# A list-scheduled attention and feed-forward kernel: a third engine allowed for two kinds of cast, and a new table of places

## The chip, the core and the metric

The kernel runs on one core of a Trainium2 chip. A core has a matrix engine (TensorE, PE in the rows; its weight loads are PEld), a vector engine (VectorE, DVE), a scalar engine (ScalarE, ACT), GpSimd (POOL), and SyncE (SP), which here only issues DMAs. Each engine works through its own list of instructions in order; semaphores tie the lists together. The metric is the device time of one execution in microseconds (us), the median of several. A profiled execution gives a trace, and its span (first to last instruction) is a little shorter than its device time.

## What is computed

```python
scores = q @ k.T / 8                    # 8 batches x 8 heads, 576 tokens, 64 wide
# heads 0-3 keep the 32 tokens up to their own, heads 4-7 every 32nd token
attn = softmax(where(mask, scores, -1e9)) @ v
x = attn.transpose(0, 2, 1, 3).reshape(4608, 512)
h = x @ w_in                            # 512 x 2048
out = (h * sigmoid(h)) @ w_out          # 2048 x 512
```

## The kernel before, in words

Attention is split per batch into six groups: groups 0 to 2 hold tiles of the local heads, 3 to 5 tiles of the strided heads. A group's steps are: load of keys and queries (`k`), scores on PE (`S`), masked copy with the row's peak on DVE (`M`, line 574), exponential on ACT (`E`, 583 or 595), row sums and scaling on DVE (`R`, `N`), a turn on PE and a copy back on ACT (`T`, `P`), the product with the values on PE (`O`), and the copy of its result into x on ACT (`B`, 686 or 703). In later batches the turn is done by a DMA with two 16-bit copies ahead of it (`X`) and two behind it (`Z`), which any of DVE, ACT and POOL may make (lines 638 and 648).

The feed-forward part keeps float32 accuracy with pairs of fp32r numbers, an upper part and a remainder. The weights come as 32 pieces of 512 KB (16 of w_in, 16 of w_out, taken in turn). A piece costs one load `p`, two ACT passes that round it (`a`, lines 434 and 439), a joining DVE pass (`j`, 445), a cast of the upper part (`b`, 481), and a DVE subtraction for the remainder (`d`, 485). x gets the same: a cast of each of its four quarters (`H`, 722) and a subtraction (`L`, 727). The first three blocks of 512 tokens are multiplied straight (`h` and `o`, lines 735 and 782); the other six go in three pairs by a scheme with fewer products, whose combined operands DVE and ACT make (products at lines 1598 and 1637).

Nobody writes the order of the instructions down. Each piece of work is a `Step` with a cost for every engine that may do it and a due time. `Steps.arrange` (line 294) simulates the engines: among the steps that can begin next it takes the one with the earliest due time, and of the engines that a step may use, the one on which it would end first. The order found is the order of every engine's list. Two tables correct it: `SHIFT` adds to the due time of single steps, `GIVEN` pins single steps to one engine. The order of the DMA issues on SP comes out of the same due times, so the first loads can be read from the code: due of a `k` load of batch 0, group c, is -1 + 2.2c, of a `v` load 6 + 2.2c, of a weight load 14 + 6.4(fc + 1.4 layer), each plus its entry in `SHIFT`; the earliest is issued first.

Of the kernel before, what the change touches and what calls it, by code (L numbers as in the profile page):

```python
# [25 lines left out]
B, H, S, D = 8, 8, 576, 64  # L26
# [48 lines left out]
class Group:  # L75
# [50 lines left out]


SHIFT = {
# [52 lines left out]
}  # L181
GIVEN = {
# [5 lines left out]
}  # L188


# [159 lines left out]
def sparse_attention_ffn(ctx: ExitStack, tc: tile.TileContext, kqt, vt, w_in, w_out, out, out_t):  # L350
# [453 lines left out]
    add = steps.add  # L804
    state = {}

    def do(*args, **kwargs):
        return steps.do(*args, **kwargs)
# [173 lines left out]
    def piece_steps(i):  # L982
        layer, fc = pieces[i]
        due = begin + (fc + layer * 1.4) * pace - 4
        lent_to = []
        if fc in cuts[layer][0]:
            lent_to = [lent[key] for half in range(2) if (key := (layer, half, fc)) in lent]
        if i % AHEAD < LENT and i < 2 * (NFC - LENT):
            where = f"stage{i % AHEAD}"
        else:  # L990
            where = f"ring{next(turns) % (AHEAD - LENT)}"
        p = add(f"p{i}", {"SP": 512 * P * 8 / RATE}, due - 6, [], lambda: load_piece(i),
                writes=[where])
        a = add(f"a{i}", {"ACT": 1.18}, due, [p], lambda: round_weights(stages[i]))
        j = add(f"j{i}", {"DVE": 0.7}, due + 0.5, [a], lambda: join_weights(stages[i]))
        h = add(f"b{i}", {"DVE": 0.46, "ACT": 0.57}, due + 1, [j],
                lambda: high(i, h.engine), writes=lent_to)
        d = add(f"d{i}", {"DVE": 0.66}, due + 1.5, [h], lambda: low(i))
        steps.reads(d, where)
        return d  # L1000
# [2 lines left out]

    def x_steps(k, cc, after=(), due=None):
        more = 0.2 * (((k + 1) * T - 1) // S - k * T // S)
        high = do(f"H{k}{cc}", {"ACT": 0.52 + more, "DVE": 0.5 + more},
                  lambda: x_high(k, x, cc, high.engine), writes=[("x", cc)], after=after, due=due)
        low = do(f"L{k}{cc}", {"DVE": 0.68 + 0.5 * more},
                 lambda: x_low(k, x, cc, low.engine), writes=[("x", cc)], due=due)
        return high, low  # L1010
# [878 lines left out]
```

## Time and profile before

| | |
|---|---|
| time, median of 3 runs | 816.59 us (815.8 to 817.57) |
| the profiled execution | 814.57 us, span 812.8 us |
| PE busy in the span | 795.9 us (98%) |
| DVE, ACT, POOL busy | 571.2, 474.1, 58.8 us |
| DMA | 190.21 MB, mean 234 GB/s |

Busy time of PE is the time in which a product was under way; its pauses are the span less that. The stretches and single rows that matter are in the section of rows below.

### The profile page before, as it was taken

The numbers are of one execution on the slowest core, as the hardware profiler recorded it, in microseconds if no ns is written. First come the engines' busy times: TensorE is split into PE (matmuls) and PEld (weight loads), VectorE is DVE, ScalarE is ACT, GpSimd is POOL, SyncE is SP. The second block draws the span as 40 slices with busy tenths as digits, with TensorE's granted clock in tenths as the row PEclk, the third lists the DMA queues.
The fourth block names the chain that finished last, engine by engine and source line by source line (L and its number), as shares of the span: only waits on it lengthen the run. The fifth ranks groups of instructions, "written<-read, shape, count | busy, mean of one in ns | idle before, by whom it ended". The sixth has DMA issues, their size and how long they took to land.

```text
span 812.8 us, 17610 instructions
## 1 busy us (share of the span) xinstructions
PE 795.9 (98%) x6900; PEld 655.7 (81%) x6900; DVE 571.2 (70%) x1370; ACT 474.1 (58%) x1160; POOL 58.8 (7%) x67
## 2 busy tenths in 40 slices
PE   5899999999999999999999999999999999999997
PEld 4788888888888888887888888888888888888886
DVE  6999876768988988843898866237867640379662
ACT  7988754636566656777678554555545344455440
POOL 2000000012100112100221100000000000000000
PEclk9999999999999999999999999999999999999999
DMA  9898988878776888889887778665585675555662
GB/s 330 298 299 243 243 237 257 254 212 241 223 236 181 251 257 251 243 256 264 275 269 257 257 263 278 198 220 182 184 230 187 238 244 177 194 207 191 205 225 103
DMA packets 112979, 190.21 MB, mean 234 GB/s; under 512 B 42880, under 2 KB 87424, under 8 KB 102144
## 3 DMA queue, kind: packets, MB, share of 16 engines
q1 hardware_dynamic: 112896, 189.08, 73.3%
q8 instruction: 54, 0.88, 0.4%
q14 instruction: 29, 0.24, 0.1%
HBM read 141.08 MB, written 38.80 MB: 221 GB/s over the span
## 4 chain that ended last, share of the span: by engine, by line
PE 95%; DMA 2%; ACT 2%; DVE 0%; SPq 0%; issue 0%; DVEq 0%
PE z L1637 28%; PE z L1598 27%; PE po L782 16%; PE ph L735 16%; PE pa L555 3%; PE ph L668 1%; DMA w<-ops 1%; PE z L668 1%; DMA w<-kqt 1%; PE pa L668 1%; ACT stage L434 0%; ACT stage L439 0%; PE po L668 0%; SPq L492 0%; ACT xhi L722 0%; ACT pt L618 0%
## 5 line engine op out<-in xcount | busy, mean ns | idle before, releaser
L1598 PE MATMUL z<-w,w 128*128 128x512 f32 x720 | 166.5, 390 | 0.8 <-DMA w<-ops 0.8
L1598 PEld LDWEIGHTS z<-w,w 128*128 128x128 f32 x720 | 134.8, 188 | 29.3 <-issue 1.2
L1637 PE MATMUL z<-w,w 128*128 128x512 f32 x576 | 133.9, 389 | 0.0
L1637 PEld LDWEIGHTS z<-w,w 128*128 128x128 f32 x576 | 108.0, 188 | 22.5
L735 PE MATMUL ph<-xhi,w 128*128 128x512 f32 x384 | 123.8, 392 | 0.0
L583 ACT ACTIVATE sm<-sm,sums 128x64 f32<-128x64 f32 x304 | 101.5, 340 | 9.2 <-DVE sums L574 8.2
L782 PE MATMUL po<-w,g 128*128 128x512 f32 x432 | 104.3, 392 | 0.0
L782 PEld LDWEIGHTS po<-w,g 128*128 128x128 f32 x432 | 80.3, 188 | 17.4 <-DVE g L762 0.5
L1464 DVE TENSOR_TENSOR w<-w,w 128x1024 fp32r<-128x1024 f32 (+3 forms) x68 | 78.3, 1162 | 12.2 <-ACT w L1535 9.6
L735 PEld LDWEIGHTS ph<-xhi,w 128*128 128x128 f32 x384 | 72.3, 188 | 15.4
L735 PE MATMUL ph<-xlo,w 128*128 128x512 f32 x192 | 75.0, 390 | 0.0
L1493 DVE TENSOR_TENSOR w<-w,z 128x1024 f32<-128x1024 f32 x30 | 36.5, 1218 | 37.4 <-PE z L1598 37.3
L1535 ACT CAST w<-w 128x1024 fp32r<-128x1024 f32 (+1 forms) x40 | 39.2, 987 | 35.5 <-PE z L1637 34.1
L583 ACT ACTIVATION_READ_ACCUMULATOR sm<-sm,sums 128x1 f32 x304 | 58.6, 193 | 0.0
L1481 ACT ACTIVATE w<-w 128x1024 f32<-128x1024 f32 x30 | 31.8, 1062 | 39.8 <-DVE w L1493 39.7
L648 POOL COPY pt<-sm 128x896 uint16<-128x896 uint16 (+1 forms) x21 | 28.7, 1375 | 322.9 <-DMA sm<-pt 233.4
L1637 PE MATMUL z<-xhi,w 128*128 128x512 f32 x216 | 52.0, 390 | 0.0
L1637 PE MATMUL z<-xlo,w 128*128 128x512 f32 x216 | 52.0, 390 | 0.0
L1487 ACT COPY w<-z 128x1024 f32<-128x1024 f32 x30 | 30.4, 1014 | 35.5 <-PE z L1598 35.4
L745 ACT ACTIVATE th<-ph 128x512 f32<-128x512 f32 x48 | 28.5, 593 | 37.3 <-DVE g L762 24.2
L1637 PEld LDWEIGHTS z<-xhi,w 128*128 128x128 f32 x216 | 40.5, 188 | 8.5
L1637 PEld LDWEIGHTS z<-xlo,w 128*128 128x128 f32 x216 | 40.5, 188 | 8.4
(169 smaller groups left out, 1173.3 us busy)
## 6 DMA issues: line engine op xcount, KB each, us to landing
w<-ops SPq DMA_DIRECT2D x84, 1024.0 KB, 4.9
ops<-stage SPq DMA_DIRECT2D x48, 256.0 KB, 3.1
kd<-kqt SPq DMA_DIRECT2D x23, 448.0 KB, 5.6
ops<-w SPq DMA_DIRECT2D x80, 128.0 KB, 4.2
vd<-vt SPq DMA_DIRECT2D x24, 384.0 KB, 6.0
stage<-w_out SPq DMA_DIRECT2D x16, 512.0 KB, 5.3
stage<-w_in SPq DMA_DIRECT2D x16, 512.0 KB, 6.4
kd<-kqt SPq DMA_DIRECT2D x14, 442.0 KB, 5.5
```

Of the source, the lines that this page charges most:

```text
L583: nc.scalar.activation(out=self.s_sb[:, c, r], in_=self.s_sb[:, c, r], func=AF.Exp, bias=self.nmax[:, c, r : r + 1], scale=-1.0, accum_out ...
L648: copy[engine](out=self.halves(self.pt)[:, half], in_=came[:, half])
L735: nc.tensor.matmul(ph, weight(0, wi, fc)[:, cc * P : (cc + 1) * P], x[xi][:, cc], start=(cc, n) == (0, 0), stop=(cc, n) == (NP - 1, 2),)
L745: nc.scalar.activation(out=th[:, cols], in_=ph[:, cols], func=AF.Tanh, scale=0.5)
L782: nc.tensor.matmul(po[tt], g[gi][:, cols], weight(1, wi, fc), start=fc == 0 and n == 0, stop=fc == NFC - 1 and n == 2,)
L1464: nc.vector.tensor_tensor(out=o, in0=x, in1=y, op=op1)
L1481: nc.scalar.activation(out=o, in_=x, func=AF.Silu)
L1487: nc.scalar.copy(out=o, in_=x)
L1493: nc.vector.tensor_add(o, x, y)
L1535: nc.scalar.copy(out=hi, in_=x)
L1598: nc.tensor.matmul(zt[z][:, jj], w[:, at, wi, cc * P : (cc + 1) * P], op[:, xi, cc], start=fresh and (cc, n) == (0, 0), stop=(cc, n) == (1 ...
L1637: nc.tensor.matmul(zt[zz][:, ds], w[:, at, wi, ds * P : (ds + 1) * P], op[:, gi, jj], start=fresh and (jp, jj, n) == (0, 0, 0), stop=(jp, ...
```

## The change

The casts of the weights' upper parts (`b`, 32 steps) and of x (`H`, 12 steps) may now go to POOL as well; the schedule takes 0.95 us and 0.9 us (plus a little where a block crosses batches) for them there. Steps with two operands are not offered to POOL. `SHIFT` and `GIVEN` are replaced as a whole, so nearly every step may stand at another place. What the schedule does not hold is any cost of one engine's work to another engine.

```diff
 SHIFT = {
...
-    "j2": 237, "j21": 1761.5, "k": -132.5, "k0.0": -132.5, "k1.1": -7497.23, "k10.1": 121, "k12.3": 231,
-    "k13.1": 229.5, "k14.2": 247, "k14.5": 275.5, "k15.0": 277, "k16.4": 309, "k2.2": -7499.41,
-    "k20.5": -337.5, "k21.0": -300, "k21.3": -138, "k22.4": -123, "k23.2": -163, "k3.3": -6873,
-    "k4.4": -34, "k5.5": -7513.5, "k6.3": -37, "k7.1": 19.5, "k7.4": 60.5, "k8.5": 75.5, "k9.0": 144.5,
...
-    "o7": 161.5, "p1": -132, "p10": 30.5, "p11": -2.5, "p12": 51.5, "p13": 47.5, "p14": 46.5, "p15": 56,
...
-    "p4": -144.5, "p5": -48.5, "p8": 44.5, "plain0.0.A110": -47.5, "plain0.0.A120": -44,
...
+    "E6.4": 2299, "E7.6": 2354, "H12": 2338.5, "L01": 2089.5, "L12": 2246.5, "L13": 1556,
+    "M1.1": 1646.5, "M1.2": 1687, "M19.1": 2259.5, "M19.3": 2210.5, "M19.4": 2259.5, "M19.5": 2224.5,
...
+    "h12": -427.5, "h13": -418, "h14": -428.5, "h2.6": -562.5, "h2.7": 208.5, "i1.15": -477,
...
+    "j8": 2362, "j9": 2403.5, "k": -2836.5, "k0.0": -1354.5, "k1.1": -1393.5, "k10.1": 70, "k10.4": 117,
+    "k13.1": 202, "k15.3": -247.5, "k16.1": 393, "k2.2": -2911.5, "k21.3": -72.5, "k3.3": -1581,
+    "k4.4": -339.5, "k5.5": -1011, "k6.0": -224, "k6.3": -183.5, "k7.1": -333, "k7.4": -185,
...
+    "l2.10": 2353, "l2.5": -348, "l8": 1858, "o1.11": -502.5, "p0": -202, "p1": -1306, "p10": -114.5,
+    "p11": -89, "p12": -121, "p16": 54.5, "p17": 39, "p2": -408, "p20": 45.5, "p21": 38, "p23": 33,
+    "p24": 38.5, "p3": -186, "p4": -335.5, "p5": -179.5, "p6": -138, "p7": -281, "p8": -196.5,
+    "p9": -147.5, "plain0.0.A110": -278, "plain0.0.A111": -299, "plain0.0.A220": 46.5,
...
+    "q1.3": -345, "s0.1": 274, "s0.2": 265, "t1.3": 2159, "v0.0": -263.5, "v1.1": -374, "v12.0": 283,
...
+    "v3.3": -215, "v4.4": -228, "v5.5": -366, "v7.1": -134, "w1.15": -770, "w15": 2316, "w2.0": -376.5,
...
 }
 GIVEN = {
-    "H02": "DVE", "H13": "ACT", "H23": "DVE", "X13.1": "ACT", "X16.0": "ACT", "X19.0": "ACT",
-    "X6.1": "POOL", "X7.0": "ACT", "Z12.0": "POOL", "Z12.1": "POOL", "Z14.0": "ACT", "Z16.0": "DVE",
-    "Z18.0": "DVE", "Z6.0": "ACT", "b16": "DVE", "b17": "ACT", "b18": "ACT", "b19": "ACT", "b2": "ACT",
-    "b20": "ACT", "b23": "ACT", "b26": "ACT", "b5": "ACT", "b8": "DVE", "w2": "ACT", "w2.10": "ACT",
-    "w2.2": "DVE", "w3": "ACT", "w5": "DVE",
+    "H01": "POOL", "H13": "POOL", "X11.1": "ACT", "X13.0": "ACT", "X14.1": "ACT", "X15.0": "POOL",
+    "X16.0": "POOL", "X6.1": "POOL", "X7.0": "ACT", "X7.1": "ACT", "Z17.1": "POOL", "b0": "POOL",
+    "b12": "POOL", "b13": "ACT", "b19": "ACT", "b27": "POOL", "b3": "POOL", "b31": "POOL", "b4": "DVE",
+    "b8": "ACT", "b9": "ACT", "w1.0": "DVE", "w2": "ACT",
 }
...
-        h = add(f"b{i}", {"DVE": 0.46, "ACT": 0.57}, due + 1, [j],
+        h = add(f"b{i}", {"DVE": 0.46, "ACT": 0.57, "POOL": 0.95}, due + 1, [j],
                 lambda: high(i, h.engine), writes=lent_to)
...
-        high = do(f"H{k}{cc}", {"ACT": 0.52 + more, "DVE": 0.5 + more},
+        high = do(f"H{k}{cc}", {"ACT": 0.52 + more, "DVE": 0.5 + more, "POOL": 0.9 + more},
                   lambda: x_high(k, x, cc, high.engine), writes=[("x", cc)], after=after, due=due)
```

## Rows read from the trace of the kernel before

**Rows 1.** Busy time by stretch (stretch, its length, each engine's busy time and instructions, clock, DMA).
```profile
0.00:6.40 6.40, 1.89 (x72) 1.46 (x72) 0.02 (x1) 1.28 (x1) 4.74 (x24) 1.00 0.61 206
6.40:14.00 7.60, 3.86 (x131) 2.89 (x131) 6.56 (x64) 6.85 (x38) 0.00 (x0) 1.00 1.04 377
14.00:20.00 6.00, 5.39 (x93) 4.11 (x96) 5.63 (x22) 6.00 (x18) 0.00 (x0) 1.00 1.06 399
20.00:32.80 12.80, 10.14 (x280) 8.42 (x275) 12.18 (x39) 12.26 (x30) 0.00 (x0) 1.00 0.84 281
40.00:100.00 60.00, 60.00 (x552) 49.06 (x551) 55.08 (x149) 50.00 (x136) 2.88 (x2) 1.00 0.91 265
100.00:380.00 280.00, 279.97 (x3025) 230.87 (x3023) 213.26 (x684) 171.87 (x564) 31.57 (x26) 1.00 0.81 240
380.00:382.00 2.00, 1.20 (x6) 0.72 (x5) 1.22 (x1) 0.10 (x1) 0.00 (x0) 1.00 0.93 264
382.00:808.20 426.20, 426.20 (x2731) 352.31 (x2729) 269.69 (x389) 219.28 (x356) 19.65 (x15) 1.00 0.66 219
```
**Rows 2.** Timeline of PE: start, duration, instruction, idle time before and what ended it.
```profile
4.06 0.92 PE L555 MATMUL pa<-w 64*64 64x64 f32 x24 [4.06 <-DMA w<-kqt]
5.35 0.97 PE L555 MATMUL po<-kd 64*32 64x64 f32 x48 [0.36 <-DMA kd<-kqt]
...
29.75 1.12 PE L668 MATMUL po<-pt,w 64*64 64x54 f32 x32 [1.05 <-ACT pt L618]
30.79 2.03 PE L555 MATMUL pa<-kd 64*32 64x64 f32 x80
32.76 0.79 PE L735 MATMUL ph<-xhi,w 128*128 128x512 f32 x1
...
381.41 1.86 PE L1598 MATMUL z<-w,w 128*128 128x512 f32 x7 [0.80 <-DMA w<-ops]
```
**Rows 3.** The chain that ended last, 13 to 30 us (start, duration, what).
```profile
17.52 0.56 ACT stage L434
18.08 0.57 ACT stage L439
...
25.10 0.55 ACT w L481
...
27.56 0.62 ACT xhi L722
...
29.21 0.49 ACT pt L618
```
**Rows 4.** Timelines of POOL, DVE and ACT at the start.
```profile
0.96 2.27 POOL L390 TENSOR_SCALAR_AFFINE_SELECT mask_local<-mask_local 32x64 f32<-32x64 f32 x8
...
6.38 0.22 DVE L574 CUSTOM_DVE_ANT_0 sm<-pa,mask_strided 128x64 f32<-128x64 f32 x1 [6.38 <-POOL mask_strided L390]
...
6.64 0.35 ACT L583 ACTIVATE sm<-sm,sums 128x64 f32<-128x64 f32 x1 [4.63 <-DVE sums L574]
```
**Rows 5.** DMA issues of the first 40 us: KB each, median us from issue to landing.
```profile
kd<-kqt SPq DMA_DIRECT2D x5, 448.0 KB, 5.9
...
w<-kqt SPq DMA_DIRECT2D x1, 334.0 KB, 3.3
...
stage<-w_in SPq DMA_DIRECT2D x7, 512.0 KB, 8.5
```
**Rows 6.** Groups of casts, 6.4 to 32.8 us (count, busy us, mean ns of one, idle before).
```profile
L481 ACT CAST w<-stage 128x512 fp32r<-128x512 f32 x3 | 2.0, 663 | 0.0
L722 ACT CAST xhi<-xb 128x512 fp32r<-128x512 f32 x3 | 1.9, 619 | 0.1
...
L481 DVE CAST w<-stage 128x512 fp32r<-128x512 f32 x3 | 1.3, 426 | 0.1
L722 DVE CAST xhi<-xb 128x512 fp32r<-128x512 f32 x1 | 0.4, 419 | 0.0
```
**Rows 7.** Copies on POOL: durations ns min/median/max, and one small copy.
```profile
L638 POOL COPY pt<-sm x22: 827/1172/2026, 53.0 to 522.4; 128x896 uint16<-128x896 uint16 x15, 128x768 uint16<-128x768 uint16 x7
...
3.30 0.24 POOL L403 COPY mask_first<-mask_local 128x72 f32<-128x72 f32 x1
```
**Rows 8.** DVE beside a POOL copy (timelines), and one DVE line's durations min/median/max.
```profile
107.24 1.29 POOL L648 COPY pt<-sm 128x768 uint16<-128x768 uint16 x1 [13.84 <-DMA sm<-pt]
107.53 1.49 DVE L485 TENSOR_TENSOR stage<-stage,stage 128x512 fp32r<-128x512 f32 x1
...
L762 DVE TENSOR_TENSOR g<-th,g x48: 629/691/1520, 39.3 to 321.7; 128x512 fp32r<-128x512 f32 x48
```
**Rows 9.** Casts of weights, 33 to 130 us, by engine.
```profile
L481 ACT CAST w<-stage 128x512 fp32r<-128x512 f32 x13 | 8.5, 659 | 0.6 <-DVE stage L445 0.6
...
L481 DVE CAST w<-stage 128x512 fp32r<-128x512 f32 x10 | 4.2, 424 | 0.2
```

77 rows, old and new, of the table SHIFT are left out of this document.

## The prediction

> **What bounds the kernel now.** I read the busy time by stretch first, because the shares of a whole span hide where an engine waits. From 32.8 us to 808.2 us PE pauses only once for long, 0.80 us at 381 us for a load [rows 1, 2]; all other stretches there are busy to within 0.03 us. The products themselves are not touched by this change, so they cannot get shorter. What can get shorter is the time in which PE waits: the span less its busy time is 812.8 - 795.9 = 16.9 us. Of this, 32.8 - (1.89 + 3.86 + 5.39 + 10.14) = 11.5 us lie before the first big product at 32.76 us [rows 1, 2], 0.8 us at 381 us, and 4.6 us behind the last product, where nothing of the change has a place. So the question is what sets the start of the big products.
>
> The first 4.06 us are the wait for the first load [rows 2]. Behind it, ACT and DVE are both nearly full: ACT 6.00 of 6.00 us and 12.26 of 12.80, DVE 5.63 and 12.18 [rows 1]. The chain of work that ended last says which of the two counts more. It lies on ACT for most of 13.2 to 29.7 us: roundings, a weight cast, casts of x, and last the copy of 29.21 us, for which PE waits 1.05 us before the last batch-0 attention product at 29.75 us [rows 2, 3]. POOL has nothing to do from 6.4 us to beyond 32.8 us [rows 1].
>
> **The change, part by part.** *Casts that leave ACT and DVE.* Between 6.4 and 32.8 us there are six casts on ACT and four on DVE [rows 6]. One of the six, a weight cast, starts at 32.43 us, too late to matter. A cast keeps ACT for 0.55 us (25.10 us in the chain; its 0.66 us overlaps its neighbour), and DVE for 0.43 us [rows 3, 6]. The table pins b0, b3 and H01 to POOL and b4 to DVE; the others go where they would end first, and with both other engines over 95% full that will often be POOL although it is slower. I take six of the ten: four from ACT, 4 x 0.55 = 2.2 us, two from DVE, 0.85 us. Ends: three and nine.
>
> *What a cast costs on POOL.* No row of before has a 512-wide float32 copy there. The nearest are 0.24 us for 72 wide and 0.83 us for the quickest 768-wide 16-bit copy [rows 7]; on the line between, 512 wide takes 0.24 + 440 x 0.59/696 = 0.61 us. Float32 at twice the stride may be slower: the upper end is the median of the 16-bit copies, 1.17 us, some of which were held back. I take 0.8 us, nearer to the lower end, whose rows nothing held back. Against ACT's 0.55 us that is up to 0.25 us more on one dependence, hidden where the next step waits for ACT anyway. [...]
>
> *What POOL does to DVE.* At 107.53 us a DVE subtraction of two operands takes 1.49 us, where that line's neighbours take 0.69: it began 0.29 us after a POOL copy and ended only after it [rows 8]. The same happens to the line with 48 instructions, 0.691 us in the median and 1.520 at worst [rows 8]. So a POOL copy can hold DVE back by anything from nothing to 0.83 us. I take 0.4 us a cast, halfway, since a copy may start at any point of a DVE instruction: 6 x 0.4 = 2.4 us on DVE. The schedule counts none of this. [...]
>
> *The order of the first loads.* Before, group 5 came first; it needs the mask for strided heads, for which DVE waits until 6.38 us, though PE had begun at 4.06 us [rows 2, 4]. By the new due times the order is k2, k (first tile of group 0), k3, k1, k0, v2, p1, k5. Group 2 needs only the local mask, finished at 0.96 + 2.27 = 3.23 us [rows 4]. Its load is 114 KB bigger than group 5's [rows 5], 0.3 us at 377 GB/s [rows 1], so PE begins at about 4.4 us, its 48 products take 0.97 us [rows 2], and DVE and ACT begin about 1.0 us earlier. The loads behind come no faster, since the DMA engines were full before too (1.04 and 1.06 of their time [rows 1]), so some of this runs into waits for data: I take 0.7 us on both engines. Ends: 0 and 1.6 us.
>
> *Together before 32.8 us.* ACT: -0.7 - 2.2 = -2.9 us. DVE: -0.7 - 0.85 + 2.4 = +0.85 us. The chain lies on ACT far more than on DVE, but DVE is close behind; I weigh them 0.8 to 0.2: -2.3 + 0.2 = -2.1 us for the start of the stream.
>
> *The stream, 33 to 130 us.* Here 23 more weight casts are made on w, 10 of them on DVE [rows 9]. If some 13 go to POOL, five of them from DVE, DVE gets 13 x 0.4 - 5 x 0.43 = +3.1 us. It has 4.9 us free between 40 and 100 us alone [rows 1], so I count nothing; without that cover (13 x 0.83 - 2.1 = 8.7 us, against 4.9) PE would wait 3.8 us. The new places of all later steps I cost at nothing too: after 100 us DVE is busy 213 of 280 us and ACT 172 [rows 1], and PE hides them; the 0.80 us at 381 us may go or double, with no row that says which.
>
> **Sum.** 812.8 - 2.1 = 810.7 us of span. The profiled execution's own time was 814.57, so 812.5 us there; the median of the runs lies 2.0 us above the profiled one, and 816.59 - 2.1 gives 814.5 us.
>
> **Rivals.** *Both engines freed.* If POOL takes nine casts (five of ACT, 2.7 us, and all four of DVE, 1.7 us) and finds gaps on DVE, ACT is 0.7 + 2.7 = 3.4 us earlier, or 4.3 us with all of the 1.6 us of the first loads; about 4 us gives 812.6 us. For it: POOL is empty. Against: DVE leaves few gaps.
>
> *DVE takes the bound (slower).* Place: DVE's two-operand passes before 32.8 us and up to 100 us. At 0.6 us a cast, six casts put DVE 3.6 - 1.55 = 2.05 us later before the stream, and in it 13 casts cost 7.8 - 2.1 = 5.7 us, 0.8 us more than DVE has free: +2.9 us, 819.4 us, once the chain has moved to DVE. At the worst price, 0.83 us, it is 3.4 + 3.8 = +7.2 us. It decides where DVE's delay before the stream is zero, 1.55/6 = 0.26 us a cast, if DVE sets the start alone, and at some 0.58 us, where the free time is used up, if ACT does. For it: the 1.49 us row; against: the median of that line in the trace stays at 0.69 us.
>
> *The loads set the start, and the change hides.* The piece of w_in that the first product needs lands late: issued at 15.36 us before, with 8.5 us to landing [rows 5] that is near 24 us, and in the new order p0 stands behind a like amount of data. Three microseconds of rounding, joining, cast and subtraction follow, so before 27 us nothing can start; PE then still has the last attention and the next scores to do, 1.12 + 2.03 us [rows 2], which it does in any order. If attention also waits for its values, a gain of -0.5 us stays: 816.1 us. That is also where the change would end if few casts moved.
>
> **Chances.** A difference under 0.2% (1.6 us) is about what a measurement of this kernel cannot tell from none. My forecast (-1.0 to -3.2 us) 0.42, of which 0.35 is over 0.2%; both freed 0.14; loads 0.20, of which 0.03 is a gain over 0.2%; DVE bound 0.24, of which 0.19 is over 0.2% slower. Faster 0.52, same 0.29, slower 0.19. The range from 811.5 to 818.5 us reaches from the second-best part of "both freed" to the milder part of "DVE bound" and leaves out under 2 in 10; the forecast's own range is 813.4 to 815.6 us.
>
> **What would show it.** Right: POOL casts of about 0.8 us between 17 and 32 us, fewer casts on ACT there, DVE's first mask before 5.6 us, the first big product at 30 to 31.5 us, PE without pauses behind it, DVE passes of 1.0 to 1.5 us beside POOL casts. Wrong: big products that start at 32.5 us or later, pauses of PE between 40 and 130 us that end with a DVE subtraction, or a longer wait near 381 us.

## The result: 820.44 us, slower by half a per cent

The changed kernel takes 820.44 us (median of 6 runs, 819.43 to 823.06). The kernel before took 816.58 us beside it. The ratio is 1.0054, 95% interval [1.0041, 1.0066]: slower, where 814.5 us and a gain had been forecast. The profiled execution took 820.87 us, its span is 818.7 us.

Below `GIVEN` all line numbers are ten lower than before: the cast of a weight is L471 (was L481), of x L712 (722), the subtractions L475 and L717, the first product of the stream L725, the gate passes of the feed-forward part L739 and L752. Kernels built from before keep the old numbers.

Busy time by stretch, the columns as in [rows 1]:

```profile
0.00:6.40 6.40, 1.18 (x64) 0.94 (x64) 1.04 (x13) 2.06 (x6) 4.74 (x24) 1.00 0.67 195
6.40:14.00 7.60, 4.27 (x139) 3.40 (x139) 5.80 (x50) 6.02 (x31) 0.00 (x0) 1.00 1.04 388
14.00:20.00 6.00, 5.38 (x143) 4.75 (x135) 5.57 (x22) 6.00 (x21) 1.77 (x2) 1.00 0.85 328
20.00:32.80 12.80, 8.11 (x200) 6.40 (x197) 9.99 (x33) 8.74 (x23) 2.69 (x3) 1.00 0.92 313
40.00:100.00 60.00, 59.95 (x477) 48.78 (x476) 54.09 (x141) 44.56 (x124) 8.57 (x9) 1.00 0.86 270
100.00:380.00 280.00, 275.61 (x3074) 225.91 (x3073) 222.44 (x683) 165.73 (x542) 42.85 (x42) 1.00 0.78 236
380.00:382.00 2.00, 2.00 (x11) 1.65 (x10) 0.00 (x0) 2.00 (x13) 0.84 (x1) 1.00 0.79 287
382.00:812.00 430.00, 429.77 (x2747) 355.23 (x2745) 270.86 (x389) 230.99 (x369) 19.85 (x14) 1.00 0.65 221
```

PE's busy time is 795.7 us, as before. Its pauses are 818.7 - 795.7 = 23.0 us, where they were 16.9 us [rows 1]. The 6.1 us more are: up to 32.8 us 13.86 instead of 11.52 us (+2.3); from 100 to 380 us 280 - 275.61 = 4.39 instead of 0.03 us (+4.4); the wait at 381 us is gone (-0.8); 0.2 us behind that. These are two single executions. The one of before lies 2.0 us below its median and this one 0.4 above, so 6.1 us of the profiles stand for 3.9 us of the medians.

Where the pauses are, in the timeline of PE:

```profile
27.01 1.12 PE L658 MATMUL po<-th,w 64*64 64x54 f32 x32 [3.91 <-DMA w<-vt]
...
33.93 0.50 PE L725 MATMUL ph<-xhi,w 128*128 128x512 f32 x1
...
42.27 2.88 PE L772 MATMUL po<-w,g 128*128 128x512 f32 x12
...
117.16 0.55 PE L658 MATMUL pa<-pt,vd 64*64 64x32 f32 x24 [0.38 <-ACT th L735]
127.77 0.50 PE L725 MATMUL ph<-xlo,w 128*128 128x512 f32 x1 [0.56 <-DVE xlo L717]
163.93 0.56 PE L658 MATMUL ph<-pt,vd 64*64 64x54 f32 x21 [1.16 <-issue]
214.02 0.50 PE L725 MATMUL ph<-xhi,w 128*128 128x512 f32 x1 [0.57 <-DVE th L739]
239.20 0.50 PE L725 MATMUL ph<-xhi,w 128*128 128x512 f32 x1 [0.54 <-DVE th L739]
321.88 0.50 PE L725 MATMUL ph<-xhi,w 128*128 128x512 f32 x1 [1.19 <-DVE th L739]
```

The first big product starts at 33.93 us, 1.17 us later than before [rows 2]. The block of 36 products that it opens ends at 42.27 us, 0.71 us later than before (41.56 us): here the products stand 0.23 us apart from the second on, while in before the first two took 0.59 and 0.42 us. The longest wait before the first big product, 3.91 us, is for values of batch 0. The chain that ended last says why they are late, and the waits of SP's queue confirm it:

```profile
16.17 1.19 POOL w L471
...
17.39 1.12 DVE w L475
...
18.56 0.38 SPq L460
...
18.98 0.86 SPq L489
...
19.88 6.99 DMA w<-vt
```

```profile
SPq L460 <- DVE w L475: 6.9, 1, 6.9
```

SP issues the loads in the order of its list: L460 at 18.56 us, and only then, at 18.98 us, L489. At 11.6 us SP comes to the load of weight piece 7 (L460), whose buffer DVE gives back only with the subtraction for piece 1, at 18.51 us. Two loads of values (L489) stand behind it. The DMA engines run dry meanwhile: from 19 to 20 us they are busy for 0.26 of the time, where it was 1.07 in before. Two windows of after, then the same two of before (DMA share and GB/s are the last columns):

```profile
18.00:19.00 1.00, 1.00 (x50) 1.00 (x44) 1.00 (x2) 1.00 (x6) 0.00 (x0) 1.00 0.63 246
19.00:20.00 1.00, 1.00 (x44) 1.00 (x40) 0.93 (x5) 1.00 (x3) 0.00 (x0) 1.00 0.26 72
```

```profile
18.00:19.00 1.00, 1.00 (x44) 1.00 (x44) 0.96 (x3) 1.00 (x4) 0.00 (x0) 1.00 1.07 409
19.00:20.00 1.00, 0.68 (x27) 0.54 (x26) 1.00 (x6) 1.00 (x5) 0.00 (x0) 1.00 1.07 419
```

Three of the later pauses end with the same DVE instruction, L739. DVE and POOL ahead of the one at 214 us:

```profile
208.39 0.69 DVE L1149 TENSOR_TENSOR stage<-w,w 128x512 f32<-128x512 f32 x1 [1.43 <-DMA ops<-stage]
209.11 0.42 DVE L1159 TENSOR_TENSOR stage<-stage 128x256 f32<-128x256 f32 x1
...
210.03 1.40 DVE L1161 TENSOR_TENSOR stage<-stage 128x256 f32<-128x256 f32 x1
...
212.28 1.09 DVE L595 TENSOR_TENSOR sm<-sm,sums 128x896 f32<-128x896 f32 x1
213.29 0.68 DVE L739 SCALAR_TENSOR_TENSOR th<-th,ph 128x512 f32<-128x512 f32 x1
```

```profile
210.00 1.20 POOL L638 COPY pt<-sm 128x896 uint16<-128x896 uint16 x1 [4.88 <-DMA sm<-pt]
```

DVE waits 1.43 us until a store empties a buffer, then makes sums for the product scheme. One of them takes 1.40 us instead of 0.42, from 0.03 us behind the start of a 16-bit join on POOL to 0.23 us behind its end. Only then comes the gate pass that PE needs. Nothing in this chain is a cast on POOL: the join, `Z12.0`, was pinned to POOL in the old `GIVEN` too and stands at another moment now. In all, POOL makes 46 of the 16-bit copies, where it made 43.

### The profile page after: what moved, and what is told of

It reads as the page before. It is cut to its first block, busy times and chain, and to the rows that moved or that the text cites. A ratio compares the mean times of both kernels' runs of the same rounds, so it can differ in the third digit from the quotient of the medians.

```text
span 818.7 us, 17658 instructions
## 1 busy us (share of the span) xinstructions
PE 795.7 (97%) x6900; PEld 654.4 (80%) x6900; DVE 578.1 (71%) x1361; ACT 473.3 (58%) x1145; POOL 82.0 (10%) x95
## 4 chain that ended last, share of the span: by engine, by line
PE 78%; DVE 11%; DMA 4%; ACT 3%; issue 2%; SPq 0%; POOL 0%; DVEq 0%; ACTq 0%; POOLq 0%
PE z L1627 28%; PE z L1588 26%; PE po L772 10%; PE ph L725 9%; PE pa L545 3%; DMA ops<-stage 2%; ACT sm L573 1%; DVE th L739 1%; PE ph L658 1%; DVE stage L435 1%; DMA w<-vt 1%; DVE w L475 1%; DVE g L752 1%; PE z L658 1%; DVE stage L1177 1%
## 5 line engine op out<-in xcount | busy, mean ns | idle before, releaser
L725 PE MATMUL ph<-xhi,w 128*128 128x512 f32 x384 | 123.9, 392 | 2.3 <-DVE th L739 2.3
L725 PEld LDWEIGHTS ph<-xhi,w 128*128 128x128 f32 x384 | 72.1, 188 | 18.9 <-DVE th L739 3.6
L725 PE MATMUL ph<-xlo,w 128*128 128x512 f32 x192 | 75.0, 391 | 0.6 <-DVE xlo L717 0.6
L735 ACT ACTIVATE th<-ph 128x512 f32<-128x512 f32 x48 | 28.6, 596 | 50.1 <-DVE g L752 34.3
L638 POOL COPY pt<-sm 128x896 uint16<-128x896 uint16 (+1 forms) x24 | 33.5, 1408 | 188.4 <-DMA sm<-pt 140.5
L628 POOL COPY pt<-sm 128x896 uint16<-128x896 uint16 (+1 forms) x22 | 25.1, 1155 | 251.7 <-PE z L658 131.0
```

The source lines that it names most:

```text
L638: copy[engine](out=self.halves(self.pt)[:, half], in_=came[:, half])
L725: nc.tensor.matmul(ph, weight(0, wi, fc)[:, cc * P : (cc + 1) * P], x[xi][:, cc], start=(cc, n) == (0, 0), stop=(cc, n) == (NP - 1, 2),)
L735: nc.scalar.activation(out=th[:, cols], in_=ph[:, cols], func=AF.Tanh, scale=0.5)
```

## The experiments

Each ratio is to before, run on the same chip. In the kernels built from after's order, "e1's list" means the change of the first experiment. Each run has the profile of one execution, and that can lie 1.6 us below the run's median (runs 5 and 7) or 2.2 us above it (run 8), so the pauses of a profile need not be those of the median.

**1. The blocked load moved back.** After, with piece 7's load behind the last loads of values; every other list unchanged.

```diff
+    order = steps.arrange()
+    held = steps["p7"]
+    order.remove(held)
+    order.insert(order.index(steps["v3.3"]) + 1, held)
```

> The changed kernel with one DMA issue moved in SyncE's list and nothing else: the load p7, which waits for its stage buffer until the weight piece 1 has been split, is issued behind the values v4 and v3 of batch 0 and no longer ahead of them. If the new places cost the time at the start (a blocked load holds up the loads behind it and the DMA engines run dry), the wait of 3.9 us for the values shrinks to 1 to 2 us, the first big product comes 2 us earlier than 33.9 us, and the time falls to about 818.3 us. If GpSimd's hold on VectorE sets the start, VectorE is as late as before and the time stays within 0.5 us of 820.4.

Measured: 818.49 us, 1.0037 [1.0021, 1.0054]. SP now issues the values at 12.35 us, and the wait for them is gone:

```profile
12.35 2.53 SPq L489 DMA_DIRECT2D w<-vt  x2
18.62 0.38 SPq L460 DMA_DIRECT2D stage<-w_in  x1
```

```profile
31.97 0.79 PE L725 MATMUL ph<-xhi,w 128*128 128x512 f32 x1
```

The big products start 0.8 us earlier than in before, yet the kernel stays slower: the pauses from 100 to 380 us remain (2.97 us there). Against after, the first big product is 1.96 us earlier and the end of its block 1.43 us (40.84 us), since the first two products again took 0.59 and 0.43 us. The median falls by 1.95 us, but the two intervals overlap.

**2. A fill in place of the cast.** After, with zeros written by POOL where it cast, so that it reads nothing; upper parts of those pieces and quarters are zero.

```diff
-            copy[engine](out=weight(layer, 0, fc), in_=stages[i][:, :, 1].bitcast(F32))
+            nc.gpsimd.memset(weight(layer, 0, fc).bitcast(F32), 0.0)  # POOL only; x alike
```

> The changed kernel with all lists in the same order, but each cast of a weight's upper part or of x that stands on GpSimd is a fill with zeros of the same place: it reads nothing, so the upper parts made there are zero and the remainders are the whole numbers. If GpSimd's reads hold VectorE back enough to cost the time, VectorE's subtractions beside them come back to 0.69 us and the time falls by 3 us or more, to 817.5 or less. If the new places cost the time, only the 0.3 to 0.7 us a cast on its own chain goes, and the time falls by 0.5 to 1.5 us, to 819 to 820.

Measured: 819.48 us, 1.0042 [1.0031, 1.0054]. First big product 33.62 us; 3.12 us of pauses from 100 to 380 us. Beside the fills alone DVE's passes are 0.02 us longer in all, and DVE is busy 573.27 us of the first 812 us, where it was 576.82 us in after, so the edit does what it is for. What POOL reads in its casts is not the main cause.

**3 and 4. One half of the change each, order planned anew.** The new tables without POOL casts, and the old tables with them.

```diff
-{"DVE": 0.46, "ACT": 0.57, "POOL": 0.95}
+{"DVE": 0.46, "ACT": 0.57}                  # 3, new tables
...
-{"DVE": 0.46, "ACT": 0.57}
+{"DVE": 0.46, "ACT": 0.57, "POOL": 0.95}    # 4, old tables; H alike in both
```

> The new table of places, but the casts of weights and of x may not go to GpSimd (their seven pins are dropped with it), so VectorE and ScalarE make them. If GpSimd's casts cost the time, this comes to 816.6 or less. If the places cost it, it stays at 819 or more; with the casts back on two full engines it may be slower than 820.4.

> The old table of places and pins, but the casts of weights and of x may go to GpSimd where the schedule likes it. If GpSimd's casts cost the time, this is slower than 816.6 by 2 us or more. If the new places cost it, this stays within 1.5 us of 816.6, or is faster by the 1 to 2 us that I forecast for the start.

Measured: 845.03 us, 1.034 [1.0321, 1.0359], and 851.46 us, 1.0437 [1.0418, 1.0455]. Both are far worse than either kernel. Planned with the other set of engines, a table gives an order in which PE pauses 8.2 and 19.2 us from 100 to 380 us. So these two do not separate the halves. The next two keep an order fixed and move only engines.

**5. After's order, its 20 casts on ACT.**

```diff
+        if step.engine == "POOL" and re.match(r"(b\d+|H\d+)$", step.name):
+            step.engine = "ACT"
```

> The changed kernel's lists, with each of the 20 casts that stand on GpSimd made by ScalarE at the same place of the order; nothing else moves. If GpSimd's casts are what costs the time, through their hold on VectorE, the subtractions beside them come back to 0.69 us and the time falls to 818 us or less. If the new places cost it, the stalls stay, ScalarE gets 20 x 0.55 us more to do, and the time is 820 us or more.

Measured: 820.27 us, 1.0053 [1.0038, 1.0069]: as slow as after, with no cast on POOL. The profile, though, does not show the stalls of after, as was expected if the places cost the time:

```profile
32.39 0.79 PE L725 MATMUL ph<-xhi,w 128*128 128x512 f32 x1
...
34.26 0.63 PE L725 MATMUL ph<-xlo,w 128*128 128x512 f32 x1
34.69 1.05 PE L725 MATMUL ph<-xhi,w 128*128 128x512 f32 x2
```

```profile
100.00:380.00 280.00, 278.66 (x3088) 228.67 (x3087) 221.50 (x686) 172.94 (x569) 36.41 (x30) 1.00 0.79 240
```

Piece 7's load is blocked as long as in after (it is issued at 18.33 us), but PE waits only 0.20 us for the values, its first big product comes 1.54 us earlier than in after, and from 100 to 380 us it pauses 1.34 us instead of 4.39. Some of this is lost again: the products stand 0.43 us apart until 35.54 us, so that the first block ends at 42.26 us, as in after (42.27 us); and PE pauses 1.18 us at 578 us, where after pauses 0.23. What is left, 1.8 us of span, is about what this profile lies below the run's median. So the median says that the casts do not make the loss; which pauses make it in an execution at the median, this run does not show.

**6. Before's order, the same 20 casts on POOL.**

```diff
+    moved = {"b0", "b1", "b2", ..., "H21", "H22"}   # the 20
+        if step.name in moved:
+            step.engine = "POOL"
```

> The kernel before with its own lists, but the same 20 casts (14 of weights, 6 of x) made by GpSimd at the place where VectorE or ScalarE made them. This is the one part of the change without any new place. If GpSimd's casts cost the time, it is slower than before by 2 us or more, with pauses of TensorE between 33 and 130 us. If only the places cost it, it stays within 1 us of 816.4.

Measured: 816.37 us, 1.0004 [0.999, 1.0017]: no difference. Windows, and PE's first big product and one long pause:

```profile
100.00:380.00 280.00, 279.63 (x3023) 230.11 (x3021) 213.49 (x679) 167.94 (x552) 38.90 (x38) 1.00 0.79 240
380.00:382.00 2.00, 0.66 (x3) 0.43 (x3) 1.22 (x1) 0.49 (x1) 0.00 (x0) 1.00 0.83 253
```

```profile
32.14 0.79 PE L735 MATMUL ph<-xhi,w 128*128 128x512 f32 x1
...
381.56 2.78 PE L1598 MATMUL z<-w,w 128*128 128x512 f32 x11 [1.34 <-DMA w<-ops]
```

The start gains 0.6 us and the wait at 381 us grows by 0.5 us. Runs 5 and 6 together settle the first question, within the 0.2% or so of their intervals: moved at a fixed order, the casts on POOL neither make the loss nor gain anything that can be measured; the places make the loss.

**7. Four joins off POOL.** e1's list, with four joins of the turn by DMA on ACT.

```diff
+    for name in ("Z12.0", "Z13.1", "Z17.0", "Z17.1"):
+        steps[name].engine = "ACT"
```

> The kernel with the one load moved behind, and the four 16-bit joins that stand on GpSimd just ahead of TensorE's pauses at 212, 237 and 319 us made by ScalarE. If GpSimd's hold on VectorE is what makes VectorE late there (its sums of 0.43 us took 1.2 to 1.4 us), the three pauses, 0.53 + 0.70 + 0.48 us, go and the time falls from 818.5 to about 816.8 us. If the store for which VectorE waits first (landing at 208, 233 and 317 us) is enough by itself, they stay.

Measured: 817.41 us, 1.0022 [1.0008, 1.0035]. The pauses at 237 and 319 us are gone, the one at 211 us stays (0.61 us); 1.40 us are lost from 100 to 380 us. DVE's and ACT's rows ahead of the one that stays:

```profile
207.42 0.42 DVE L1161 TENSOR_TENSOR stage<-stage 128x256 f32<-128x256 f32 x1
...
210.60 0.69 DVE L739 SCALAR_TENSOR_TENSOR th<-th,ph 128x512 f32<-128x512 f32 x1 [0.81 <-ACT th L735]
```

```profile
208.90 1.21 ACT L638 COPY pt<-sm 128x896 uint16<-128x896 uint16 x1
```

Without the join on POOL the sum takes 0.42 us and not 1.40. But the join now stands on ACT, ahead of the tanh (L735, 209.98 us) that the gate pass needs, and DVE waits 0.81 us for that. The edit took away one cause of this pause and put another in its place.

**8. The gate passes ahead of the sums.** e1's list, with the two gate passes of each of three products moved ahead of the sums that they stood behind.

```diff
+    for k, fc, late in ((1, 12, "sums0.4"), (2, 0, "sums0.6"), (2, 13, "sums1.6")):
+        ...                        # t and g of k.fc go ahead of `late`
```

> The kernel with the one load moved behind, and at the same three pauses the gate and its tanh stand ahead of the sums of weights on VectorE and ScalarE; the joins stay on GpSimd. If the place of the gate behind sums that wait for a store costs the time, the three pauses go as well and the time is about 816.8 us, though VectorE's sums are still held to 1.2 us. If VectorE is late as a whole, the pauses move to the next gate and the time stays at 818.5 us.

Measured: 818.32 us, 1.0037 [1.0024, 1.005], as e1. The three pauses behind L739 near 212, 237 and 319 us are gone and others stand there (0.86 us at 163, 0.18 at 225, 0.52 at 327, 0.41 at 339): 3.2 us are lost from 100 to 380 us. Moving a pass by hand moves the hole.

**9. The blocked load in before's list.**

```diff
+    held = steps["p7"]
+    order.remove(held)
+    order.insert(order.index(steps["v4.4"]), held)
```

> The kernel before, with one thing changed: on SP the load of piece 7 is issued one place ahead of the load of v4.4 instead of behind the load of piece 3 (three loads earlier). Theory that a blocked load holds back the loads behind it: piece 7 waits on SP until DVE is done with piece 1, about 21.4 us, so v4.4, k6.0 and piece 3, which before issued at 16.29 to 21.39 us, start only behind it; the DMA engines lose some of 17 to 22 us, the last values land at 27 us or later (before 24.45), the first big product comes at 33.5 to 35 us (before 32.76) and the time is 1.001 to 1.003 of before. Rival (the loads in the list have slack, the start is set by ACT and DVE): first big product within 0.3 us of before, time 0.999 to 1.001.

Measured: 815.32 us, 0.9997 [0.9984, 1.0011]; first big product 32.44 us. The rival is right here. SP's queue shows that the load was blocked all the same. The first row below takes two loads together, piece 7's as the second; 6.31 us less 0.38 us for each issue is a wait of 5.5 us:

```profile
15.02 6.31 SPq L470 DMA_DIRECT2D stage<-w_in  x2
21.37 0.56 SPq L499 DMA_DIRECT2D w<-vt  x1
```

But the values behind it were not yet needed: PE's last wait before the stream is 1.05 us for ACT's copy (L618), as in before. The wait of 5.5 us did not make the start of the big products later here (32.44 us, in before 32.76 us).

**10 and 11. The two kernels cut at the second big product and joined crosswise.** The steps up to there in the order and on the engines of one kernel, the rest as in the other.

```diff
+    for item in first:             # the other kernel's first 138 (140) steps
+        name, engine = item.split(":")
+        step = steps[name]
+        step.engine = engine
+        rest.remove(step)
+        order.append(step)
+    order += rest
```

> The 138 steps that the changed kernel places ahead of its second big product stand in its order and on its engines; all other steps in the order and on the engines of the kernel before (so only the start's casts are on GpSimd). Theory (loss in two parts: loads held behind piece 7 at the start, joins and gates placed badly later): first big product at 33.5 to 34.2 us, no pauses at 212, 237 and 320 us, 1.002 to 1.003 of before. Rival (the start's loss is absorbed or given back later): 1.000 to 1.001. Rival (all of the loss is at the start): 1.004 to 1.006.

> The counterpart: the 140 steps that the kernel before places ahead of its second big product stand in its order and on its engines, all others in the order and on the engines of the changed kernel. Two parts: first big product at 32.1 to 32.9 us, pauses near 212, 237 and 320 us still there, none at 381 us, 1.002 to 1.0035 of before. If all of the loss is at the start: 0.999 to 1.001. If all of it is in the later places: 1.004 to 1.006.

Measured: new start, old rest 821.07 us, 1.0071 [1.0053, 1.0089]; old start, new rest 821.54 us, 1.0075 [1.0056, 1.0094]. Both above what any theory gave, because the seam itself opens a pause just behind it, which neither parent has (the second row of each fence). PE's rows and the window of 10, then of 11:

```profile
25.76 1.01 PE L668 MATMUL po<-th,w 64*64 64x54 f32 x28 [3.39 <-DMA w<-vt]
...
43.41 0.79 PE L735 MATMUL ph<-xhi,w 128*128 128x512 f32 x1 [2.68 <-DVE th L749]
```

```profile
100.00:380.00 280.00, 280.00 (x3100) 230.92 (x3099) 218.08 (x691) 169.65 (x556) 31.79 (x26) 1.00 0.81 240
```

```profile
29.14 1.11 PE L658 MATMUL po<-pt,w 64*64 64x54 f32 x32 [1.05 <-ACT pt L608]
40.44 0.50 PE L725 MATMUL ph<-xhi,w 128*128 128x512 f32 x1 [1.48 <-DVE th L739]
```

```profile
100.00:380.00 280.00, 275.43 (x3070) 225.10 (x3069) 221.18 (x682) 165.33 (x538) 42.79 (x41) 1.00 0.78 237
```

Less the pauses of the seams (2.68 and 1.48 us) it is 2.5 us for the new start and 4.2 us for the new later places, by medians. These are rough: behind the seam of 10, seven products take 0.41 to 0.59 us each, some 1.5 us more than at 0.23, and without these 1.0 us is left for the start. The windows say it without the seams: the wait for the values goes with the start (3.39 us in 10, none in 11), the pauses from 100 to 380 us go with the rest (0.00 in 10, 4.57 in 11).

**12. A try at a faster kernel.** Run 6, with two stores put behind the next transposing load on SP, so that they do not share the DMA engines with the load that PE awaits at 381 us.

```diff
+    for name in ("ws1.7.1", "s2.2"):
+        held = steps[name]
+        order.remove(held)
+        order.insert(order.index(steps["Y20"]) + 1, held)
```

> The kernel before with the 20 casts on GpSimd as in the earlier run with the old places, and on SP two stores of 256 KB each (the ones issued at 372.46 and 372.94 us there) put behind the transposing load that follows the next operand load. Theory (PE's wait of 1.34 us at 381 us is for an operand load of 1024 KB that shares the DMA engines with the two stores): without them the load lands 1 to 2 us earlier, the wait goes, and with the start of the big products at 32.1 to 32.8 us the time is 0.998 to 0.9995 of before, a version that beats both kernels if the interval stays below 1. Rival (the time of the stores is only moved to the next load, or the tiles that they empty hold ACT and DVE back): a pause of about 1 us appears somewhere in 382 to 395 us and the time is 0.9995 to 1.002.

Measured: 815.81 us, 1.0002 [0.9993, 1.0012]. The wait is gone (the window below), the first big product starts at 32.24 us, and still nothing is won:

```profile
380.00:382.00 2.00, 2.00 (x10) 1.66 (x9) 0.48 (x1) 0.00 (x0) 0.00 (x0) 1.00 0.74 188
...
sum 808.20, PE 796.67 PEld 655.65 DVE 567.49 ACT 466.45 POOL 77.23; mean PE 159.33 PEld 131.13 DVE 113.50 ACT 93.29 POOL 15.45
```

Three pauses of 0.1 to 0.35 us came up at 128, 222 and 235 us, and PE was busy 796.67 us up to 808.2 us, where run 6 had 795.64: the product work itself filled 1.0 us more. Product by product, it is 0.1 us behind run 6 at the first big product, 0.4 us at the end of that block, 1.9 us at 235 us, and 0.2 to 0.4 us ahead once the wait at 381 us is past. No run shows why the products took longer. No version that beats before was found.

## Why the prediction was wrong

**The step that failed** is "The new places of all later steps I cost at nothing too", with its cover "PE hides them". The cover was read from shares: DVE busy 213 of 280 us [rows 1]. The new places cost 4.39 us of PE's pauses there in the changed kernel and 4.57 us in run 11, against 0.00 us in run 10 with the old ones. All seven profiles with the new later places pause 1.34 us (run 5) to 4.57 us there, all five with the old ones 0.00 to 0.63 us. DVE was busy 222 of 280 us, so it had 58 us to spare, and was late all the same: its list is in order, and a gate pass stood behind sums that waited for a store and were held by a join. A share says how much time is free, not that the instruction PE needs next is in front.

**The order of the first loads.** Its first half was right: DVE's first mask starts at 5.36 us, 1.0 us earlier, as forecast. Its second half was not: the prediction followed the new list for its first eight loads and took the rest as unchanged. Piece 7 stood ahead of two loads of values and was blocked for 6.9 us. The forecast of 2.1 us earlier became 1.17 us later; without the block it is 0.8 us earlier (run 1). The size is uncertain, and the block alone does not make the start late: run 5 has it, and its first big product is 0.4 us earlier than in before. The load was issued at 18.3 to 18.7 us in four profiles with this order, and the wait for values was 3.91 us in after, 3.39 in run 10, 1.75 in run 2 and 0.20 in run 5.

**The casts, by themselves.** Up to 32.8 us POOL made five (forecast: six). The price was right as a mean: the 13 weight casts into w up to 130 us took 0.84 us, forecast 0.8. No single cast took that: seven took 0.65 or 0.66 us, close to the forecast's lower end, and six 1.04 to 1.18 us. Each of the six began while a DVE pass of L435, L475 or L717 was under way, and none of the seven did. So it was partly luck: beside these passes POOL's casts took longer, and that was not in the sum.

```profile
L471 POOL CAST w<-stage 128x512 fp32r<-128x512 f32 x13 | 10.9, 843 | 72.2 <-DVE stage L435 72.2
...
L712 POOL CAST xhi<-xb 128x512 fp32r<-128x512 f32 x1 | 0.6, 613 | 3.1 <-ACT xb L676 3.1
```

What POOL does to DVE was taken as 0.4 us a cast; the DVE instructions that lay beside the casts took 3.3 us longer together than the median of their line and shape, which over 20 casts is under 0.2 us each. Most of DVE's delays beside POOL (21.5 of 24.4 us; in before all of 14.1 us) lie beside the 16-bit copies. At 210 us a sum beside a copy took 1.40 us instead of 0.42. Beside the casts delays of 0.4 us came only at single places, among them three subtractions (L475 at 17.39, 26.76 and 62.88 us) with 1.10 to 1.13 us instead of 0.69.

The gain from the casts was mis-sized too. By the prediction's weights they alone give -2.2 x 0.8 + (2.4 - 0.85) x 0.2 = -1.5 us at the start; in run 6 it was -0.6 us, and 1.0004 in all.

**The rivals.** "DVE takes the bound" gave 819.4 us, nearest to 820.44, for another reason: its mechanism was POOL's casts, and run 5 without them is as slow. One of its signs did come: the pause of 0.56 us at 127.77 us ends with a subtraction of x (L717), 4 us behind six POOL casts of x at 120.09 to 123.70 us. Runs 1, 7, 8 and 11 have it as well; runs 2 and 5, in which POOL does not cast, do not. There the casts cost some 0.55 us. "The loads set the start" had the right engine with the wrong load: not the piece that the first product needs, but the values behind a blocked piece. That the piece of the first product, p0, "stands behind a like amount of data" was off: it is issued at 20.84 us, where it was 15.36, behind 19 loads instead of 17 and behind the block. The price at which DVE's free time is used up, "some 0.58 us" a cast, should be (4.92 + 2.15) / 13 = 0.54 us; nothing hangs on it. The sign "big products at 32.5 us or later" was fulfilled. "A longer wait near 381 us" was not; it went.

**What stays open.** The pause at 163.93 us (1.16 us) stands among small attention products with no releaser; it is 0.86 us in run 8, 0.21 in run 1 and not there in runs 5, 7 and 11. The parts do not add up: start and later places alone give 2.5 + 4.2 us, both together 3.9 us. A late start may also let the lists of the other engines run ahead; no run shows it. How much of the loss lies in each pause at the median stays open too, since run 5 is as slow as after with fewer pauses in its profile. Nor were all later places tried: run 7 got 1.0022 with four joins moved, and what remains lies in the start and in pauses at 116, 127, 211 and 575 us.

## What to carry to other kernels

When a table of places is replaced, read the issue list of the DMA queue to the end of the start: for each load ask which buffer it needs, when that comes free, and what stands behind it. An engine's spare share does not help an instruction that stands in an in-order list behind one that waits; look for the store, the sum or the join ahead of the pass that PE needs. Judge a start by when a later product of the same list begins, not by the first one: runs 1 and 5 started 1.96 and 1.54 us before after, and 36 products on 1.43 and 0.01 us were left. To tell an assignment from an order, hold the order fixed and change the engine: replanned halves (runs 3 and 4) lost 29 and 35 us and told nothing of the change.

## What the runs showed of the hardware beyond that

One blocked issue on SP was enough to take the DMA engines from 422 GB/s (17 to 18 us) to 72 GB/s (19 to 20 us).

The granted clock at the start was not the same in all orders. In run 1 it fell between 20 and 24 us (mean 0.87, PE busy 2.48 us of the 4) and was 0.50 from 24 to 32.8 us; in run 10 it fell there too (0.83, PE busy 1.42 us) and was 0.50 up to 36 us. In the changed kernel it stayed at 1.00, though PE was busy 2.52 us from 20 to 24 us and 0.99 us from 24 to 28 us. No run here tells what made the difference.

The spacing of the big products shows more than the clock column. In run 10 they stand 0.43 us apart from 34.45 to 36.16 us, where the granted clock is 0.50, and 0.23 us apart once it is 1.00 again. In runs 2, 5 and 11 the first ones stand 0.43 us apart as well, though the column shows 1.00 there. Whether the clock was at 0.50 in those stretches, no row says.

At some places DVE and POOL took longer beside each other. A DVE sum of two operands that began 0.03 us behind a copy on POOL took 1.40 us instead of 0.42; a cast on POOL that began 0.15 us behind a DVE subtraction of two operands (31.39 us, behind L717 at 31.24) took 1.04 us instead of 0.65. Beside three DVE passes of L739, which read `th` and `ph`, the result of PE's products (45.39, 64.54 and 105.79 us), the casts took 0.65 to 0.66 us.
